# Three edits to the opening of an attention and MLP kernel: two product groups by contraction halves, key sums as a head of ones, and fewer idle products in fp32

## Chip, cores and metric

The kernel runs on one core of one Trainium2 chip. The metric is the device time of one execution in microseconds, as the median of several executions. The profile's span is about 1.8 us shorter than that time, because it runs from the first to the last recorded instruction of one profiled execution. Times of different kernels are compared only where they were measured on the same chip in the same rounds.

In this document, TensorE is called PE, VectorE DVE, ScalarE ACT, GpSimd POOL and SyncE SP. A load is one DMA transfer. The trace lists sixteen landings for it, one for each DMA engine; it counts as landed at the last of them, and the lag of an engine is how much later it lands than the other fifteen. Start to start is the time from the start of one product to the start of the next. The granted clock is the share of PE's full clock that the trace shows; "the gate opens" is its step from half to full.

## The reference

```python
# q, k, v: (8, 8, 576, 64) fp32; w_in (512, 2048), w_out (2048, 512) fp32
q_s = softmax(q over head_dim);  k_s = softmax(k over the sequence)
kv  = einsum('bhsd,bhse->bhde', k_s, v)          # one 64x64 matrix per head
x   = einsum('bhsd,bhde->bhse', q_s, kv)         # attention output
x   = x.transpose(0, 2, 1, 3).reshape(4608, 512) # tokens x d_model
h   = x @ w_in
g   = where(h > 0, h, exp(min(h, 0)) - 1)        # ELU
out = g @ w_out                                  # (4608, 512) fp32
```

## The kernel before

The program is laid out by a list scheduler of its own: each `S.add(engine, estimate, emit, key, ...)` names what an operation reads (`R`), writes (`W`) and both (`X`), and the scheduler orders each engine's instructions and places the semaphores. One unit is half of the heads of one batch, so batch 0 is units 0 and 1, and batch 1 is units 2 and 3. The 4608 tokens form nine blocks of 512.

The start-up matters here. The q loads of units 0 and 1 go first. Then one queue carries, in this order: k and v of units 0 and 1; sixteen pieces of w_in; then w_out in six pieces, mixed with q, k and v of units 2 and 3. The last things before the final two w_out pieces are the two halves of unit 3's v.

Meanwhile PE runs *idle products*, whose results nobody reads, so that its clock gate opens before the real work:

```python
def spin(self, count, bk, after=None):
    dst = self.bank(bk)
    def mm(e):
        for _ in range(count):
            last = e.matmul(dst, self.IDLE[:, 0:128], self.IDLE[:, :], start=True, stop=True)
        return last
    ...                                     # IDLE is 128 x 512, fp16
```

Unit 0's key sums (the softmax denominator over the sequence) are products of one column, ahead of the key-value products of 128 columns:

```python
def kz_first(self, n, ps, key):             # 18 products of one column each
    ...
                e.matmul(P[:, f * 512 + 128:f * 512 + 129], ek[fs, c, :], VB[fs, 0, c, D:D + 1], ...)
    ...                                     # then DVE takes the reciprocal

def kv_first(self, n, ps, key):             # 18 products of 128 columns each
    ...
                e.matmul(P[:, f * 512:f * 512 + 128], ek[fs, c, :], v[fs, :, c, :], ...)
    ...                                     # then DVE scales by the reciprocal into MBLK
```

A first-layer *group* g is 256 columns of d_ff for one block of 512 tokens: two tiles by four contraction pieces `kc`, which is eight products. A w_in load is one `kc` for four tiles, so groups 2 and 3 share four loads. In block 0, groups 0 and 1 are already split by contraction pieces, and group 2 in two halves:

```python
def hg(self, j, g, ps, key, how, kcs=(0, 1, 2, 3)):
    if (j, g) == (0, 2):
        self.hg_mm(j, g, ps, (0, 1), key)
        kcs = (2, 3)
    self.hg_mm(j, g, ps, kcs, key)
    ...                                     # exp on ACT, min and max on POOL/ACT/DVE into GT

def program(self):
    ...
    self.spin(10, 0)
    self.q_part(0, -90); self.q_mul(0, -90, None)
    self.spin(2, 0, "expq0"); self.spin(3, 0, "rec0")
    ...
    self.tp(0, 3, -84)                      # transposes of unit 0's q
    self.spin(4, 0); self.spin(2, 0, "rec1")
    self.kz_first(0, 2, -87); self.kv_first(0, 1, -87)
    ...
    for what in (0, "2q", "3q", 1, 2, "2k", "2v", "3k", 3, "3v", 4, 5):   # the queue after w_in
        ...
```

Block 0's second layer is woven with batch 1's attention. Its key-value products, `kv([2, 3])`, are one operation of 72 products that needs k and v of both units. It reads VB, the bf16 copy of v that DVE makes half by half.

The softmax here doesn't subtract the row's maximum and nothing guards it: scores larger than these inputs give would overflow.

Of the kernel before, what the change touches and what calls it, by code (L numbers as in the profile page):

```python
# [18 lines left out]
CH = 9  # L19
# [238 lines left out]
class Gen:  # L258
# [13 lines left out]
    def alloc(self):  # L272
        nc = self.nc
        a = nc.alloc_sbuf_tensor
        self.ID = a("ID", [128, 128], F16)
        self.IDLE = a("IDLE", [128, 512], F16)
        self.W1 = a("W1", [128, 4, DFF], F32R)
        self.W2 = a("W2", [128, 16, 512], F32R)
        self.GT = a("GT", [128, 16, BLK], F32R)
        self.XT = a("XT", [128, 4, RING], F32R)  # L280
        self.ESB = [a(f"ESB{i}", [128, 1024], F32) for i in range(4)]
        self.OSB = [a(f"OSB{i}", [128, 512], F32) for i in range(4)]
        self.RAW = [{t: a(f"{t.upper()}R{i}", [128, 2, CH, D], F32) for t in "kv"}
                    for i in range(2)]
        self.RQ = [a(f"QR{i}", [128, 2, CH, D], F32) for i in range(4)]
        self.VB = [a(f"VB{i}", [128, 2, CH, D + 1], BF16) for i in range(2)]
        self.QS = [a(f"QS{i}", [128, CH, 128], F16) for i in range(2)]
        self.qsT = [a(f"qsT{i}", [128, CH, 128], F32R) for i in range(2)]
        self.MB = a("MBLK", [128, 2, 2, 128], F32R)
        self.MBLK = [self.MB[:, i, :, :] for i in range(2)]  # L290
        self.ZQ = [a(f"ZQ{i}", [128, 2, CH], F32) for i in range(2)]
        self.RZQ = [a(f"RZQ{i}", [128, 2, CH], F32) for i in range(2)]
        self.RZ = a("RZK", [128, 2, 2], F32)
        self.RZK = [self.RZ[:, i, :] for i in range(2)]
        self.SEEN = a("SEEN", [16, 4, 16], F32)
        self.PS = [nc.alloc_psum_tensor(f"PS{i}", [128, 1024], F32) for i in range(4)]
# [10 lines left out]
    def load(self, n, t, eng, key, after=(), follow=None):  # L307

        b, u, i = n // 2, n % 2, n % (4 if t == "q" else 2)
        src = self.src[t][b, :, :, :].rearrange(  # L310
            "(h uf) (p c) d -> (uf p) h (c d)", h=2, c=CH)[128 * u:128 * u + 128]
        dst = self.raw(n, t)[:, :, :, :].rearrange("p h c d -> p h (c d)")
        if t == "v" and n < 2:
            dst = self.v16(n).rearrange("p h c d -> p h (c d)")
        return self.S.add(eng, ISSUE[eng], lambda e: e.dma_start(dst, src), key,  # L315
                          W=[f"{t}R{i}"] + (self.q_res(n - 4) if t == "q" and n in (4, 5) else []),
                          dma=f"{t}{i}{eng}", nbytes=128 * 4608,
                          after=after, follow=follow, low=True, tag=f"ld {t}{n}")

# [195 lines left out]
            ek[:, :, :, :], flat.rearrange("p (h c d) -> p h c d", h=2, c=CH), AF.Exp),  # L515
            key, X=[f"kR{n % 2}"], low=True, tag=f"expk{n}")

    def v16(self, n):

        return self.raw_flat(n, "v").bitcast(BF16)[:, 0:1152].rearrange(  # L520
            "p (h c d) -> p h c d", h=2, c=CH)

    def kz_first(self, n, ps, key):

# [12 lines left out]
        S.add("dve", 170, lambda e: e.reciprocal(rz.unsqueeze(2), PV[:, :, 128:129]), key,  # L537
              W=[f"RZK{n}"], X=self.banks(ps), tag=f"rzk{n}")

    def kv_first(self, n, ps, key):  # L540

        S = self.S
        P, ek, v, rz, M = self.PS[ps], self.ek2(n), self.v16(n), self.RZK[n], self.MBLK[n]

        def mm(e):
            for c in range(CH):
                for f in range(2):
                    fs = slice(f * 64, f * 64 + 64)
                    last = e.matmul(P[:, f * 512:f * 512 + 128], ek[fs, c, :], v[fs, :, c, :],
                                    start=(c == 0), stop=(c == CH - 1))  # L550
            return last
        S.add("pe", 470, mm, key, R=[f"kR{n}", f"vR{n}"], X=self.banks(ps), tag=f"kv{n}")
        PV = P[:, :].rearrange("p (f x) -> p f x", f=2)
        for h in range(2):
            hs = slice(h * 64, h * 64 + 64)
            S.add("dve", 290, lambda e, h=h, hs=hs: e.tensor_tensor(  # L556
                M[hs, :, :].rearrange("p f (e h) -> p f e h", h=2)[:, :, :, h], PV[hs, :, h * D:h * D + D],
                rz[hs, :].unsqueeze(2).broadcast_to([64, 2, D]), ALU.mult), key,
                R=[f"RZK{n}"], W=[f"MBLK{n}{h}"], X=self.banks(ps), tag=f"M{n}")
# [66 lines left out]



    def spin(self, count, bk, after=None):

        dst = self.bank(bk)

        def mm(e):
            for _ in range(count):
                last = e.matmul(dst, self.IDLE[:, 0:128], self.IDLE[:, :], start=True, stop=True)  # L635
            return last
        gate = [[o for o in self.S.ops if o.tag == after][-1]] if after else ()
        self.S.add("pe", count * 216, mm, -5, R=["IDLE"], X=[f"b{bk}"], after=gate, tag="spin")

    def hg_mm(self, j, g, ps, kcs, key=0):  # L640
        P = self.PS[ps]
# [14 lines left out]
    def hg(self, j, g, ps, key, how, kcs=(0, 1, 2, 3)):  # L656
        S = self.S
        P = self.PS[ps]
        if (j, g) == (0, 2):
            self.hg_mm(j, g, ps, (0, 1), key)  # L660
            kcs = (2, 3)
        self.hg_mm(j, g, ps, kcs, key)
        i = self.eslot % len(self.ESB)
        self.eslot += 1
# [59 lines left out]
    def init(self):  # L724
        S = self.S
        S.add("dve", 110, lambda e: e.memset(self.ID[:, :], 0.0), -95, W=["ID"])
        S.add("gp", 300, lambda e: e.affine_select(  # L727
            self.ID[:, :], self.ID[:, :], compare_op=ALU.not_equal, fill=1.0, base=0,
            pattern=[[-1, 128]], channel_multiplier=1), -79, X=["ID"])
        S.add("dve", 300, lambda e: e.memset(self.IDLE[:, :], 1.0), -96, W=["IDLE"])  # L730
        S.add("dve", 60, lambda e: e.memset(self.RZK[0], 0.0), -90, W=["RZK0"])
        for i in range(2):
            S.add("dve", 75, lambda e, i=i: e.memset(self.VB[i][:, :, :, D:D + 1], 1.0), -8,
                  W=[f"VBone{i}"])
            S.add("dve", 270, lambda e, i=i: e.memset(self.MBLK[i].bitcast(F32), 0.0), -8,
                  W=[f"MBLK{i}", f"MBLK{i}0", f"MBLK{i}1"])

    def program(self):
# [24 lines left out]
        for s in range(4):  # L763
            gp = self.load_w1(s, -60, follow=gp)
        S.add("act", 1400, lambda e: e.activation(
            self.RZK[0], self.RZK[0], AF.Exp), -65, X=["RZK0"])
        self.spin(10, 0)
        self.q_part(0, -90)
        self.q_mul(0, -90, None)
        self.spin(2, 0, "expq0")  # L770
        self.spin(3, 0, "rec0")
        self.q_part(1, -85)
        self.q_mul(1, -85, None)
        self.exp_k(0, -80)
        self.tp(0, 3, -84)
        self.spin(4, 0)
        self.spin(2, 0, "rec1")
        self.kz_first(0, 2, -87)
        self.kv_first(0, 1, -87)
        self.tp(1, 3, -84, evac="split")  # L780
        self.exp_k(1, -83)
        self.spin(2, 0)
# [45 lines left out]
        for j in range(NBLK):  # L828
            order = [A, Bs, C, Dd]
            for g in range(8):  # L830
                self.hg(j, g, order[g % 4], key, "gp" if j or g > 2 else "act" if g == 1 else "dve",
                        (0, 1, 2, 3) if j or g > 1 else (2, 3))
                key += 1
                if (j, g) == (0, 0):
                    elem_q(1, 8, None)
                    elem_k(1, 8, "dve")
# [92 lines left out]
```

## Time and profile before

| quantity | before |
|---|---|
| time, median of 3 executions | 298.55 us (298.37 to 298.98) |
| first w_in piece lands / first first-layer product | 13.14 / 13.28 us |
| first 16 KB instruction packet | 16.15 us |
| last half of unit 3's v lands | 42.46 us |
| batch 1's key-value products start | 43.01 us |
| from there to the end of the span | 253.79 us |

The page gives the busy time of an engine, its share of the span and its count of instructions. Of the profile before:

```profile
span 296.8 us, 4398 instructions
PE 291.0 (98%) x1852; PEld 234.9 (79%) x1852; DVE 149.9 (50%) x166; ACT 153.5 (52%) x182; POOL 122.7 (41%) x133
```

PE is the bound, so only PE's order, and what PE waits for, counts. A busy PE is not yet a useful PE: idle products count as busy.

### The profile page before, as it was taken

Reading aid. Unit: us, or ns where it says so; the run is one execution under the profiler, and the core shown is the slowest. Engines: PE = TensorE matmul, PEld = TensorE weight load, DVE = VectorE, ACT = ScalarE, POOL = GpSimd, SP = SyncE. Lnnn points to the kernel's source line nnn. Section 1 sums busy time; section 2 is a strip of 40 time slices with the busy share of each in tenths; the row PEclk is TensorE's granted clock in tenths of the full one; section 3 lists DMA queues with packets and bytes.
Section 4 is the critical chain, followed back from the end, with each engine's and each line's share of the span. In section 5 each row is a group of like instructions: output and inputs, shape, how many; then the busy total and the mean of one; then the engine's idle time right before and its main releaser. Section 6 shows DMA issues by size and latency. Waiting matters only on the chain.

```text
span 296.8 us, 4398 instructions
## 1 busy us (share of the span) xinstructions
PE 291.0 (98%) x1852; PEld 234.9 (79%) x1852; DVE 149.9 (50%) x166; ACT 153.5 (52%) x182; POOL 122.7 (41%) x133
## 2 busy tenths in 40 slices
PE   8999999999999999999999999999999999999995
PEld 2678778888888888888888888888888888888883
DVE  5766942988347903792268416760661056106600
ACT  5666367953776365546554745555534354125411
POOL 8998101652287035713472138315540055005500
PEclk9999999999999999999999999999999999999999
DMA  7999988928991696049902991099003110230022
GB/s 242 322 392 390 390 277 311 389 79 113 388 212 70 220 344 136 0 136 356 194 16 55 360 254 35 3 342 196 0 0 72 41 34 0 54 71 19 0 71 71
DMA packets 36515, 49.37 MB, mean 166 GB/s; under 512 B 16656, under 2 KB 17168, under 8 KB 36496
## 3 DMA queue, kind: packets, MB, share of 16 engines
q1 hardware_dynamic: 29792, 34.29, 41.1%
q0 software_dynamic: 6320, 14.29, 15.7%
q10 hardware_dynamic: 384, 0.53, 0.5%
q8 instruction: 14, 0.23, 0.3%
q14 instruction: 5, 0.04, 0.0%
HBM read 36.70 MB, written 9.44 MB: 155 GB/s over the span
## 4 chain that ended last, share of the span: by engine, by line
PE 84%; DMA 7%; POOL 7%; issue 0%; ACT 0%; DVE 0%; POOLq 0%
PE PS L698 41%; PE PS L649 39%; DMA VR<-in_v_dram 7%; POOL W L347 3%; PE PS L579 2%; PE PS L491 2%; POOL KR L315 1%; POOL W L358 1%; POOL VR L315 1%; POOL QR L315 0%; POOL QR L750 0%; ACT OSB L712 0%; DVE VB L442 0%; PE PS L613 0%; POOL ID L727 0%
## 5 line engine op out<-in xcount | busy, mean ns | idle before, releaser
L681 DVE SCALAR_TENSOR_TENSOR GT<-ESB,PS 128x1024 fp32r<-128x1024 f32 x69 | 84.1, 1220 | 116.0 <-POOL ESB L678 115.8
L698 PE MATMUL PS<-W,GT 128*128 128x512 f32 x576 | 139.9, 393 | 0.0
L649 PE MATMUL PS<-XT,W 128*128 128x512 f32 x576 | 133.0, 390 | 0.3 <-DMA W<-in_moe_w_in_dram 0.2
L649 PEld LDWEIGHTS PS<-XT,W 128*128 128x128 f32 x576 | 107.8, 188 | 23.3 <-DMA W<-in_moe_w_in_dram 0.6
L698 PEld LDWEIGHTS PS<-W,GT 128*128 128x128 f32 x576 | 106.2, 188 | 21.2 <-DMA W<-in_moe_w_out_dram 0.3
L678 POOL TENSOR_SCALAR ESB<-ESB 128x1024 f32<-128x1024 f32 x69 | 73.2, 1068 | 102.5 <-ACT ESB L666 102.5
L666 ACT ACTIVATE ESB<-PS 128x1024 f32<-128x1024 f32 x72 | 73.9, 1028 | 51.6 <-PE PS L649 51.6
L712 ACT ACTIVATE OSB<-PS 128x512 f32<-128x512 f32 x36 | 21.3, 599 | 63.0 <-PE PS L698 62.8
L438 POOL CAST VB<-VR 128x1152 bf16<-128x1152 f32 x12 | 14.4, 1202 | 45.8 <-DMA VR<-in_v_dram 45.8
L398 DVE TENSOR_REDUCE ZQ<-QR 128x18 f32<-128x1152 f32 (+1 forms) x18 | 21.8, 1214 | 3.0 <-ACT QR L392 3.0
L412 DVE TENSOR_TENSOR QS<-QR,RZQ 128x1152 f16<-128x1152 f32 x16 | 22.0, 1385 | 0.4
L599 ACT ACTIVATE XT<-PS 128x640 fp32r<-128x640 f32 (+3 forms) x24 | 15.6, 651 | 12.3 <-PE PS L579 12.3
L432 ACT ACTIVATE KR<-KR 128x1152 bf16<-128x1152 f32 x14 | 16.2, 1156 | 6.1 <-DMA KR<-in_k_dram 6.1
L392 ACT ACTIVATE QR<-QR 128x1152 f32<-128x1152 f32 (+1 forms) x18 | 18.4, 1052 | 1.7 <-DMA QR<-in_q_dram 1.6
L425 POOL CAST qsT<-QR 128x1152 fp32r<-128x1152 f16 x12 | 13.8, 1147 | 8.7 <-DMA QR<-QS 8.7
L579 PE MATMUL PS<-qsT,MBLK 128*128 128x320 f32 (+5 forms) x56 | 12.9, 312 | 0.0
L579 PEld LDWEIGHTS PS<-qsT,MBLK 128*128 128x128 f32 x56 | 10.5, 189 | 2.5 <-DVE MBLK L556 0.2
L635 PE MATMUL PS<-IDLE 128*128 128x512 f16 x24 | 8.8, 517 | 1.5 <-DVE IDLE L730 1.5
L358 POOL DMA_DIRECT2D W<-in_moe_w_out_dram x6 | 10.0, 2365 | 0.0
L347 POOL DMA_DIRECT2D W<-in_moe_w_in_dram x16 | 10.0, 1379 | 0.0
L635 PEld LDWEIGHTS PS<-IDLE 128*128 128x128 f16 x24 | 2.8, 125 | 6.2 <-issue 3.3
L491 PEld LDWEIGHTS PS<-VB,KR 64*64 64x64 bf16 x504 | 4.7, 107 | 2.8 <-DVE GT L681 1.8
(43 smaller groups left out, 70.2 us busy)
## 6 DMA issues: line engine op xcount, KB each, us to landing
out_dram<-OSB SPq DMA_DIRECT2D x68, 128.0 KB, 3.2
QR<-in_q_dram SPq DMA_DIRECT2D x12, 576.0 KB, 8.1
KR<-in_k_dram SPq DMA_DIRECT2D x12, 576.0 KB, 5.9
VR<-in_v_dram SPq DMA_DIRECT2D x12, 576.0 KB, 6.6
W<-in_moe_w_in_dram POOLq DMA_DIRECT2D x16, 256.0 KB, 9.9
W<-in_moe_w_out_dram POOLq DMA_DIRECT2D x3, 1024.0 KB, 16.8
KR<-in_k_dram POOLq DMA_DIRECT2D x4, 576.0 KB, 13.3
VR<-in_v_dram POOLq DMA_DIRECT2D x4, 288.0 KB, 14.5
```

The lines of the kernel that those rows point to most:

```text
L347: "gp", 530, lambda e, kc=kc: e.dma_start(self.W1[:, kc, sl], w[kc, :, :, sl]), key,
L392: lambda e, part=part: e.activation(part, part, AF.Exp), key,
L398: S.add("dve", 1350 if n > 1 else 750, lambda e, z=z, src=src: e.tensor_reduce(z, src, AX.X, ALU.add), key, R=self.q_res(n) if n > 1 else ...
L412: S.add("dve", 1400, lambda e: e.tensor_tensor(qso, raw[:, :, :, :], rz, ALU.mult), key, R=qR + [f"RZQ{i}"], W=[f"QS{al}"], low=True, tag= ...
L432: S.add("act", t_act(1152, False), lambda e: e.activation(ek[:, :, :, :], flat.rearrange("p (h c d) -> p h c d", h=2, c=CH), AF.Exp), key, ...
L579: return e.matmul(P[:, f * 512:f * 512 + n_], M[:, f, :], T[:, c0:c1, f * 64:f * 64 + 64], start=True, stop=True)
L649: last = e.matmul(P[:, t * 512:(t + 1) * 512], self.W1[:, kc, tt * 128:(tt + 1) * 128], self.XT[:, kc, rc:rc + BLK], start=(kc == 0), stop ...
L666: S.add("act", t_act(1024, True), lambda e: e.activation(esb[:, :], P[:, :], AF.Exp), key, W=[f"E{i}"], X=self.banks(ps), tag=f"exp{j}.{g}")
L678: S.add("gp", 1120, lambda e: e.tensor_scalar(esb[:, :], esb[:, :], 1.0, 0.0, ALU.min, ALU.max), key, X=[f"E{i}"], tag=f"min{j}.{g}", port ...
L681: S.add("dve", t_dve(1024), lambda e: e.scalar_tensor_tensor(gt, esb[:, :], -1.0, P[:, :], ALU.add, ALU.max), key, R=[f"E{i}"], W=gw, X=se ...
L698: last = e.matmul(dst, GT[:, jj, ts * 128:(ts + 1) * 128], self.W2[:, jj, :], start=(jj == 0), stop=(jj == 15))
L712: S.add("act", t_act(512, True), lambda e: e.activation(osb[:, :], src, AF.Copy), key, W=[f"O{i}0", f"O{i}1"], X=[f"b{bk}"], tag=f"evo{jb} ...
```

## The change

The change has three parts.

1. In block 0, groups 2 and 3 both go by contraction halves: first halves of 2 and 3, then second halves of 2 and 3. Each load gets more time before it is needed.
2. Unit 0's key sums become a third "head" of v that is all ones. The 18 one-column products disappear, and the key-value products grow from 128 to 192 columns.
3. Idle products are fp32. One of them is meant to hold PE as long as four fp16 ones. Fewer instructions then hold PE about equally long: 10 + 2 + 3 become 3 long ones and 1, and 4 become 1 long one.

PE's program shrinks from 1,852 to 1,820 products.

```diff
-        self.IDLE = a("IDLE", [128, 512], F16)
+        self.IDLE = a("IDLE", [128, 512], F32)
 ...
-    def kv_first(self, n, ps, key):
+    def kv_first(self, n, ps, key, sums=False):
+        w = 3 if sums else 2
-                    last = e.matmul(P[:, f * 512:f * 512 + 128], ek[fs, c, :], v[fs, :, c, :],
+                    last = e.matmul(P[:, f * 512:f * 512 + w * D], ek[fs, c, :], v[fs, 0:w, c, :],
+        if sums:
+            S.add("dve", 170, lambda e: e.reciprocal(rz.unsqueeze(2), PV[:, :, 128:129]), key, ...)
 ...
-        if (j, g) == (0, 2):
-            self.hg_mm(j, g, ps, (0, 1), key)
-            kcs = (2, 3)
 ...
+        S.add("dve", 300, lambda e: e.memset(self.v16(0, 3)[:, 2, :, :], 1.0), -8, W=["ones"])
 ...
-        self.spin(10, 0)
+        self.spin(3, 0, long=True)
-        self.spin(2, 0, "expq0")
-        self.spin(3, 0, "rec0")
+        self.spin(1, 0, "rec0")
-        self.spin(4, 0)
+        self.spin(1, 0, long=True)
-        self.kz_first(0, 2, -87)
-        self.kv_first(0, 1, -87)
+        self.kv_first(0, 1, -87, True)
 ...
-                        (0, 1, 2, 3) if j or g > 1 else (2, 3))
+                        (0, 1, 2, 3) if j or g > 3 else (2, 3))
+                if (j, g) == (0, 1):
+                    for x in (2, 3):
+                        self.hg_mm(0, x, order[x], (0, 1), key)
```

More of the change, by code (lines that the diff above doesn't have):

```diff
@@ L315, in load @@
         return self.S.add(eng, ISSUE[eng], lambda e: e.dma_start(dst, src), key,
-                          W=[f"{t}R{i}"] + (self.q_res(n - 4) if t == "q" and n in (4, 5) else []),
+                          W=[f"{t}R{i}"] + (["ones"] if t == "v" and n == 2 else []) + (self.q_res(n - 4) if t == "q" and n in (4, 5) else []),
                           dma=f"{t}{i}{eng}", nbytes=128 * 4608,
@@ L516, in exp_k, with v16 @@
             key, X=[f"kR{n % 2}"], low=True, tag=f"expk{n}")
-    def v16(self, n):
-        return self.raw_flat(n, "v").bitcast(BF16)[:, 0:1152].rearrange(
-            "p (h c d) -> p h c d", h=2, c=CH)
+    def v16(self, n, h=2):
+        return self.raw_flat(n, "v").bitcast(BF16)[:, 0:576 * h].rearrange(
+            "p (h c d) -> p h c d", h=h, c=CH)
     def kz_first(self, n, ps, key):
@@ L538, in kz_first @@
               W=[f"RZK{n}"], X=self.banks(ps), tag=f"rzk{n}")
-    def kv_first(self, n, ps, key):
+    def kv_first(self, n, ps, key, sums=False):
         S = self.S
-        P, ek, v, rz, M = self.PS[ps], self.ek2(n), self.v16(n), self.RZK[n], self.MBLK[n]
+        P, ek, v, rz, M = self.PS[ps], self.ek2(n), self.v16(n, 3), self.RZK[n], self.MBLK[n]
+        w = 3 if sums else 2
         def mm(e):
@@ L548, in mm @@
                     fs = slice(f * 64, f * 64 + 64)
-                    last = e.matmul(P[:, f * 512:f * 512 + 128], ek[fs, c, :], v[fs, :, c, :],
+                    last = e.matmul(P[:, f * 512:f * 512 + w * D], ek[fs, c, :], v[fs, 0:w, c, :],
                                     start=(c == 0), stop=(c == CH - 1))
             return last
-        S.add("pe", 470, mm, key, R=[f"kR{n}", f"vR{n}"], X=self.banks(ps), tag=f"kv{n}")
+        S.add("pe", 730 if sums else 500, mm, key, R=[f"kR{n}", f"vR{n}"] + (["ones"] if sums else []),
+              X=self.banks(ps), tag=f"kv{n}")
         PV = P[:, :].rearrange("p (f x) -> p f x", f=2)
+        if sums:
+            S.add("dve", 170, lambda e: e.reciprocal(rz.unsqueeze(2), PV[:, :, 128:129]), key,
+                  W=[f"RZK{n}"], X=self.banks(ps), tag=f"rzk{n}")
         for h in range(2):
@@ L625, in ao_last, with spin @@
               X=self.banks(ps), tag=f"evx{b}")
-    def spin(self, count, bk, after=None):
-        dst = self.bank(bk)
+    def spin(self, count, bk, after=None, long=False):
+        dst, idle = self.bank(bk), self.IDLE[:, :] if long else self.IDLE[:, 0:256].bitcast(F16)
         def mm(e):
             for _ in range(count):
-                last = e.matmul(dst, self.IDLE[:, 0:128], self.IDLE[:, :], start=True, stop=True)
+                last = e.matmul(dst, idle[:, 0:128], idle, start=True, stop=True)
             return last
         gate = [[o for o in self.S.ops if o.tag == after][-1]] if after else ()
-        self.S.add("pe", count * 216, mm, -5, R=["IDLE"], X=[f"b{bk}"], after=gate, tag="spin")
+        self.S.add("pe", count * (864 if long else 216), mm, -5, R=["IDLE"], X=[f"b{bk}"], after=gate, tag="spin")
     def hg_mm(self, j, g, ps, kcs, key=0):
```

## The prediction

> **What bounds the kernel now.** I read the page first (PE busy 291.0 of 296.8 us, granted clock at full in all 40 slices), then the chain that ended last in order of time, PE's timeline over the first 45 us, and the DMA issues stretch by stretch. The table of stretches shows where PE has slack. Its columns are the stretch, its length, busy time and count of PE, PEld, DVE, ACT and POOL, granted clock, DMA share and GB/s.
>
> ```profile
> 19.26:33.10 13.84, 13.84 (x61) 11.16 (x61) 10.90 (x10) 9.30 (x9) 10.61 (x14) 1.00 1.31 388
> 33.10:43.01 9.91, 9.64 (x57) 7.45 (x56) 6.59 (x9) 4.49 (x6) 0.00 (x0) 1.00 1.07 361
> 43.01:296.80 253.79, 250.12 (x1596) 206.37 (x1596) 120.79 (x123) 128.21 (x151) 93.93 (x88) 1.00 0.48 136
> ```
>
> After 43 us PE never waits (the missing 3.7 us are the last store). The change touches nothing there, so its whole worth is how much earlier PE reaches that point. What decides that is in the chain (start, length, what):
>
> ```profile
> 21.10 21.36 DMA VR<-in_v_dram
> 42.46 0.02 issue
> 42.49 0.48 DVE VB L442
> 42.96 0.04 issue
> 43.01 0.77 PE PS L491 x69
> ```
>
> The second batch's key-value products at 43.01 wait for the last half of unit 3's v, which lands at 42.46: the end of the load queue (about 390 GB/s from 15 us on), not PE's work, sets that time. PE's timeline shows the opening:
>
> ```profile
> 1.46 6.16 PE L635 MATMUL PS<-IDLE 128*128 128x512 f16 x15 [1.46 <-DVE IDLE L730]
> 7.51 0.68 PE L464 MATMUL PS<-ID,QS 128*128 128x128 f16 x9
> 8.03 1.72 PE L635 MATMUL PS<-IDLE 128*128 128x512 f16 x6
> 9.67 0.38 PE L532 MATMUL PS<-VB,KR 64*128 64x1 bf16 x18
> 9.91 0.66 PE L549 MATMUL PS<-VR,KR 64*128 64x128 bf16 x18
> ...
> 13.28 1.17 PE L649 MATMUL PS<-XT,W 128*128 128x512 f32 x4
> ...
> 19.26 10.29 PE L649 MATMUL PS<-XT,W 128*128 128x512 f32 x44 [0.21 <-DMA W<-in_moe_w_in_dram]
> ```
>
> The first-layer products start at 13.28. The first piece of w_in is issued at 5.69 and takes 7.5 us, so it lands near 13.2: this start too is set by a transfer. The wait of 0.21 at 19.26 is for group 2's second contraction half. The DMA issues of four stretches explain it (issues at 5.6 to 6.2, 8.6 to 9.2 and 9.2 to 9.8 us; last, the queues at 16.0 to 16.5 us):
>
> ```profile
> W<-in_moe_w_in_dram POOLq DMA_DIRECT2D x1, 256.0 KB, 7.5
> ...
> W<-in_moe_w_in_dram POOLq DMA_DIRECT2D x3, 256.0 KB, 8.2
> ...
> W<-in_moe_w_in_dram POOLq DMA_DIRECT2D x3, 256.0 KB, 9.7
> ...
> q8 instruction: 1, 0.02, 13.9%
> ```
>
> Pieces land every 0.68 us until 16.53; the next lands at 18.52. In between, at 16.15, one 16 KB instruction packet held one DMA engine for 1.11 us. The trace's sixteen landings of that piece run from 16.55 to 17.18 for fifteen engines and 18.52 for the sixteenth; the same gap of 1.38 us stays in every later load. The last half of v is complete on fourteen engines at 41.04 and on two at 42.42 and 42.46 (a second such packet came at 36.73). The same lag makes PE's weight loads wait at 33.09 for the second piece of w_out, which landed at 33.05:
>
> ```profile
> 33.09 2.61 PEld L698 LDWEIGHTS PS<-W,GT 128*128 128x128 f32 x12 [0.33 <-DMA W<-in_moe_w_out_dram]
> ```
>
> **What the Trainium skill says.** "Runtime: NRT & Kernel Launch", section "Instruction fetch mechanics": instructions come in 16 KiB blocks of 256. The trace agrees: 14 packets of 16 KB, by the trace's count 3,704 weight loads and products on PE, 265 for each packet. The page calls the cost "mostly hidden"; here it costs the loads 1.38 us. "DMA: Bandwidth & Descriptors", "Why a DMA increments its semaphore by 16 and not by 1": sixteen engines finish independently and a transfer counts only when all have; agreed, as above. "TensorE: Matmul & The Clock Gate", Part 1: a cold array runs at 1.2 GHz until a free-running window of 3.4 us has been busy. The trace agrees: idle products follow each other at 0.427 us up to 6.98, and at 0.216 from 8.03. "FP8 and Floating Point Precision", "TensorE Precision Notes": true fp32 takes four passes; no fp32 product with four passes is in this trace.
>
> **The change part by part.**
>
> *Idle products.* Removed: the first 10, the 2 after the exponentials of q, 2 of the 3 after the reciprocal, and 4 later ones. Added: 3 plus 1 in fp32. An estimate by the skill's four passes: one cold is 4 x 0.427 = 1.71 us, so three run from about 1.5 to 6.6, one more fp16 product to 7.07, and PE idles until the transposes at 7.51. They wait for DVE's QS, so they don't move. The later one, warm, is 4 x 0.216 = 0.86, as long as the four it replaces. The fill of 128x512 keeps its element count (0.48 us). Path: 0.
>
> *Key sums as a head of ones.* Removed: 18 products of one column, 0.24 us from start to start (9.67 to 9.91). Added: the 18 products grow from 128 to 192 columns. A pair of them takes 0.055 now; 192 columns at 2.4 GHz are 0.080, so nine pairs take 0.74 against 0.24 + 0.50 = 0.74: nothing on PE. But the reciprocal (0.16) now follows the products, where before it ran beside them: MBLK and the first attention products come some 0.2 us later (11.36 to about 11.6). Their copy into XT by DVE then ends near 12.85 instead of 12.63, still before 13.28; the second unit's products (12.26 to 13.1) may slip 0.1 and also still end before the first w_in piece. The new fill of ones (576 elements, estimated 0.6 us from the 0.48 of 512) falls into DVE's 2.1 us of idle time before 4.26. Path: 0.
>
> *Groups 2 and 3 by halves.* No product added or removed. The order shows 16 products before the second half of group 2 instead of 12, so PE gets there 4 x 0.23 = 0.92 later, at about 19.6, when those weights (19.22 in the worst case) are there. That removes a start-to-start gap of 0.60 where 0.23 is normal, and 0.11 of a slow second product: 0.48 us. Group 2's exponential moves about 0.4 later, with its PSUM not needed again before 25 us.
>
> *Instruction fetch.* PE's program has 1,820 products instead of 1,852, all 32 gone in the opening. With its weight load each, that is up to 64 instructions, so the first block boundary comes about 32 products later: at 0.23 each some 5 to 7 us, near 21 to 23 us (later pieces of w_in only). The second moves from 36.7 to about 44, past the last v.
>
> *Sum.* PE runs 0.48 ahead after 20 us. But at 33.09 it waits for w_out, at 43.01 for v. If the first fetch still falls before those loads, one engine still lags 1.38, and they still land at about 33.05 and 42.46. The gain becomes waiting. Products start at 43.0 as before: 0, and I allow 0.1 for a luckier engine. 298.55 - 0.1 = 298.45.
>
> **The rivals.**
> (a) The loads come early enough and the gain stays. The wait at 43.01 costs 0.66 from start to start where the later blocks show 0.32 at the same place, so at most 0.34 + 0.48 = 0.8 us: 297.7. For it: the second fetch leaves the queue's way, and the lagging engine could be one that is ahead by up to 0.6. Against: one lagging engine is enough, and already at 33.05 there was only one. Chance 15%.
> (b) The clock gate opens later because fp32 passes, or the 0.44 us gap before the transposes, count as less busy. A further 3.4 us of cold array would make idle products, transposes and the first sums 1 to 2 us longer and the first-layer start about 0.9 late. Of that the slack behind group 2 takes 0.48: 298.8 to 299.2. For: nothing in the trace of fp32. Against: the window that opened the gate, 3.6 to 7.0, is filled in both. Chance 10%.
> (c) The later reciprocal reaches the path: first-layer start 0.1 to 0.2 late, swallowed by the same two transfers. 298.5.
>
> **Range and chances.** The runs of before spread over 0.6 us (298.37 to 298.98), more than the change I expect. The 8-in-10 range takes half of rival (a) below and half of (b) above: 298.0 to 298.9. Two per cent are 6 us; the whole opening to which the change reaches has under 1 us of PE waiting to win, and a cold array costs about as much. Within 2%: 98%.
>
> **What would show it.** Right: no PE wait near 19 us; a single instruction packet between 19 and 25 us; first-layer products still at 13.2 to 13.4; PE waiting about 0.5 us longer near 33 or 43; last v near 42.4; kv products at 43.0. Wrong: last v landing before 42 (rival a), idle or transposing products at 0.1 us spacing after 7.5 us (rival b), or a first-layer start after 13.5 (c).

## The result, and the profile after

| | before (same rounds) | after |
|---|---|---|
| median | 298.73 us | 298.61 us |
| lowest to highest of 4 fast runs each | 298.37 to 298.98 | 298.16 to 298.78 |
| ratio, 95% interval | | 0.9995 (0.9977 to 1.0012) |

Ratios are the mean time of one kernel's fast runs over that of the other's in the same rounds, so they are not quite the ratio of the medians quoted. The change is within 2%, and no difference between the two kernels is resolved. The measured 298.61 us lies in the predicted range of 298.0 to 298.9, and 0.16 us above the predicted 298.45. The runs of one kernel spread over 0.6 us, so that closeness is partly luck: what the result supports is "no change", not the 0.1 us of gain.

The page of the changed kernel:

```profile
span 297.0 us, 4343 instructions
PE 289.8 (98%) x1824; PEld 234.7 (79%) x1824; DVE 150.7 (51%) x167; ACT 153.5 (52%) x182; POOL 123.0 (41%) x133
```

PE is 1.2 us less busy and the span is not shorter. The trace counts 28 fewer products where the program has 32 fewer. PE's timeline of the opening shows why. The columns are start, length from first to last, engine, line, operation, output and inputs, shapes, count and the idle time before.

```profile
1.46 4.35 PE L640 MATMUL PS<-IDLE 128*128 128x512 f32 x6 [1.46 <-DVE IDLE L732]
6.35 0.39 PE L640 MATMUL PS<-IDLE 128*128 128x512 f16 x1 [0.54 <-DVE RZQ L401]
7.75 0.68 PE L464 MATMUL PS<-ID,QS 128*128 128x128 f16 x9 [1.00 <-DVE QS L412]
...
10.05 0.92 PE L550 MATMUL PS<-VR,KR 64*128 64x192 bf16 x18
...
13.82 1.17 PE L654 MATMUL PS<-XT,W 128*128 128x512 f32 x4
16.58 13.17 PE L654 MATMUL PS<-XT,W 128*128 128x512 f32 x56
```

Three fp32 idle products are six records in the trace. While cold, each record took 0.853 us, so one product took 1.71 us. The key-value products of 192 columns stand where the sums were. The first-layer products then run from 16.58 to 29.75 in one piece: the wait at 19.26 of before is gone from this list. Start to start, small gaps of 0.328 and 0.307 us remain at group 4, where 0.23 is normal.

The first-layer start is later: 13.82 against 13.28. The chain that ended last, in order of time, then goes through the same load as before:

```profile
21.15 21.47 DMA VR<-in_v_dram
42.62 0.02 issue
42.65 0.48 DVE VB L442
43.13 0.04 issue
43.17 0.78 PE PS L491 x67
```

The last half of unit 3's v lands at 42.62 (42.46 before), DVE converts it, and the key-value products start at 43.17 (43.01 before). The table of stretches (stretch, length, then busy time and count of PE, PEld, DVE, ACT and POOL, granted clock, DMA share, GB/s) closes the account:

```profile
33.10:43.17 10.07, 9.86 (x56) 7.46 (x55) 6.79 (x9) 4.49 (x6) 0.00 (x0) 1.00 1.05 355
43.17:297.00 253.83, 250.16 (x1596) 206.40 (x1596) 120.47 (x123) 128.20 (x151) 94.09 (x88) 1.00 0.47 136
```

The stretch after the key-value products takes 253.83 us (253.79 before) with the same 1596 products. PE is busy 9.86 of 10.07 us ahead of them.

One thing did move. The first 16 KB instruction packet came at 17.78 us instead of 16.15, and the second at 42.02 instead of 36.73. The list of DMA queues of the changed kernel from 17.5 to 18 us has it (queue: packets, MB, share of the time):

```profile
q8 instruction: 1, 0.02, 14.4%
```

The lag of one DMA engine behind the others moved with the first packet. In the profile before it appears at w_in piece 7, complete on 15 engines at 17.18 and on the last at 18.52. In the changed kernel it appears at piece 9: 19.06 and 20.10.

### The profile page after: what moved, and what is told of

The parts are those of the page before. It is cut to its first block, busy times and chain, and to the rows that moved or that the text cites. A ratio compares the mean times of both kernels' runs of the same rounds, so it can differ in the third digit from the quotient of the medians.

```text
span 297.0 us, 4343 instructions
## 1 busy us (share of the span) xinstructions
PE 289.8 (98%) x1824; PEld 234.7 (79%) x1824; DVE 150.7 (51%) x167; ACT 153.5 (52%) x182; POOL 123.0 (41%) x133
## 4 chain that ended last, share of the span: by engine, by line
PE 84%; DMA 7%; POOL 7%; issue 0%; ACT 0%; DVE 0%; POOLq 0%
PE PS L700 41%; PE PS L654 39%; DMA VR<-in_v_dram 7%; POOL W L347 3%; PE PS L584 2%; PE PS L491 2%; POOL KR L315 1%; POOL W L358 1%; POOL VR L315 1%; POOL QR L315 0%; POOL QR L753 0%; ACT OSB L714 0%; DVE VB L442 0%; PE PS L618 0%; POOL ID L729 0%
## 5 line engine op out<-in xcount | busy, mean ns | idle before, releaser
L640 PE MATMUL PS<-IDLE 128*128 128x512 f32 (+1 forms) x14 | 7.4, 632 | 2.0 <-DVE IDLE L732 1.5
L640 PEld LDWEIGHTS PS<-IDLE 128*128 128x128 f32 (+1 forms) x14 | 2.5, 199 | 5.8 <-DVE RZQ L401 2.2
```

## The experiments

The theory: the key-value products of batch 1 start at the later of two times, the landing of the last half of unit 3's v plus about 0.55 us, and the time that PE itself needs from the first first-layer product. None of the three parts moves the later of the two. The main rival: the parts do change something, but their effects cancel (for example, a gain from the halves against a loss from the later start or from the clock gate).

Twelve runs were made in two sets, each set on one chip; e10 repeats after, e11 repeats e1 and e12 repeats before. The kernel before had a median of 299.06 us in the first set (e1 to e4) and 298.94 us in the second (e5 to e12). Medians of different sets are not compared. All results passed the comparison with the reference. That includes e5 and e6, which were computed from wrong data; so the comparison does not see that data, or tolerates it.

All profiled executions fit in one table. "PE's own" is the time from the first first-layer product to the key-value products. "Wait" is the start-to-start gap ahead of the key-value products, which is 0.32 where nothing is waited for. In e7 and e9, the key-value start is that of unit 2's own products.

| run | 1st instr. packet | first-layer start | last v lands | kv start | wait | PE's own | kv to end | median us |
|---|---|---|---|---|---|---|---|---|
| before | 16.15 | 13.28 | 42.46 | 43.01 | 0.66 | 29.73 | 253.8 | 298.73 |
| after | 17.78 | 13.82 | 42.62 | 43.17 | 0.60 | 29.35 | 253.8 | 298.61 |
| e1 halves | 17.99 | 16.03 | 42.45 | 44.69 | 0.32 | 28.66 | 254.0 | 298.75 |
| e2 idle products | 19.84 | 16.71 | 42.22 | 45.34 | 0.32 | 28.63 | 253.9 | 298.95 |
| e3 ones | 17.48 | 13.96 | 42.97 | 43.51 | 0.58 | 29.55 | 254.0 | 298.81 |
| e4 more idle | 14.94 | 13.82 | 42.59 | 43.13 | 0.62 | 29.31 | 254.0 | 298.89 |
| e5 light, before | 16.44 | 13.73 | 41.09 | 42.38 | 0.32 | 28.65 | 253.8 | 298.18 |
| e6 light, after | 17.21 | 13.69 | 41.22 | 42.70 | 0.32 | 29.01 | 253.8 | 298.25 |
| e7 split, after | 17.35 | 13.67 | 42.35 | 42.59 | 0.32 | 28.92 | 254.1 | 298.54 |
| e8 no idle, after | 20.37 | 14.66 | 41.84 | 43.32 | 0.32 | 28.66 | 254.0 | 299.00 |
| e9 split, before | 17.05 | 13.51 | 42.10 | 42.42 | 0.32 | 28.91 | 254.0 | 298.35 |
| e10 after again | 17.78 | 13.60 | 42.21 | 42.76 | 0.64 | 29.16 | 253.8 | 298.73 |
| e11 halves again | 16.37 | 13.30 | 42.58 | 43.13 | 0.62 | 29.83 | 253.8 | 298.71 |
| e12 before again | 16.29 | 13.25 | 42.55 | 43.09 | 0.73 | 29.84 | 253.8 | 298.69 (one run) |

Where the wait is above 0.32, the key-value products start 0.54 to 0.55 us after the landing of v. In e1, e2, e5 and e8, where it is 0.32, they start 28.63 to 28.66 us after the first first-layer product. That is PE's floor when it waits for no load on the way. In e6, e7 and e9 it is 0.32 too, but smaller gaps on the way make it 28.91 to 29.01. The intervals of the ratios are as wide as the whole prize, so the times alone could not show what a part does; the traces have to.

### e1: the halves alone

```diff
# before, with the reordering of groups 2 and 3 and nothing else (cut)
+                if (j, g) == (0, 1):
+                    for x in (2, 3):
+                        self.hg_mm(0, x, order[x], (0, 1), key)
```

> The kernel before with only groups 2 and 3 by contraction halves; idle products and key sums as before. My theory (the loads set when PE reaches 43 us): the instruction packet still comes near 16.1 us, the wait before group 2's second half (0.21 us idle, 0.48 lost) is gone, but the lagging engine now makes PE wait at group 4 (its weights land near 21.9, PE is there near 21.6), so less than 0.3 us is kept, and that is lost again at 33.05 (second piece of w_out) and before the key-value products, which start at 43.0 plus or minus 0.2. Time 298.3 to 298.9, ratio 0.999 to 1.001. Rival (PE's gain is kept): key-value products near 42.5, time near 298.1.

Measured: 298.75 us median, ratio 0.9996 (0.9977 to 1.0015). The profile fell into an unusual execution (300.51 us; the others took 298.54 to 299.01). There, the second half of unit 0's q landed at 6.27 us instead of 4.27 (fifteen DMA engines were done at 4.35, one at 6.27), and PE's timeline shows what that did:

```profile
7.03 0.61 PE L635 MATMUL PS<-IDLE 128*128 128x512 f16 x2 [1.42 <-ACT QR L392]
9.51 1.14 PE L464 MATMUL PS<-ID,QS 128*128 128x128 f16 x9 [0.36 <-DVE QS L412]
16.03 1.20 PE L649 MATMUL PS<-XT,W 128*128 128x512 f32 x4
```

PE had an idle time of 1.42 us. The granted clock, full from 5.19, was half from 8.60 to 12.01, and nine transposes took 1.14 us instead of 0.68. The first-layer products began 2.1 us after their weights had landed (13.90). This is rival (b) of the prediction in full, yet in a kernel that still has all 24 fp16 idle products. It also shows a useful limit: with PE 2.75 us late at 16.03, all waits for loads vanish and the key-value products are only 1.68 us later than in the profile before. The halves themselves could not be judged on this profile, so they were run again as e11.

### e2: the fp32 idle products alone

```diff
# shortened
-        self.IDLE = a("IDLE", [128, 512], F16)
+        self.IDLE = a("IDLE", [128, 512], F32)
-        self.spin(10, 0)           # and spin(2, "expq0"), spin(3, "rec0"), spin(4)
+        self.spin(3, 0, long=True) # and spin(1, "rec0"), spin(1, long=True)
```

> The kernel before with only the idle products changed (fp32, fewer). My theory: PE idles 0.5 to 1.0 us before the first transposes, and this costs nothing, because the first-layer products wait for the first piece of w_in (start within 0.2 us of its landing). The program is 10 pairs of weight load and product shorter, so the first instruction packet comes up to 1 us later than 16.1. Key-value products at 43.0 plus or minus 0.2, time 298.3 to 298.9. Rival (the clock gate opens later with less idle work): transposes 0.1 us apart instead of 0.056, first-layer start more than 0.4 us after the landing, time above 299.0.

Measured: 298.95 us, ratio 1.0016 (0.9979 to 1.0053). Again the profile fell on an unusual execution (301.06 us) with q late (6.42 us, fifteen engines at 4.43) and PE idle for 1.52 us; the gate closed again from 9.83 to 13.25, and first-layer products began at 16.71. The rival's symptom is there. But e1 has the same symptom without the fp32 products, and both have the late q. So this trace does not speak against the fp32 products. The other executions, at 298.74 to 298.97, do not either. The median is just above the expected 298.3 to 298.9, and the rest of the expectation (packet up to 1 us later, key-value products near 43.0) could not be judged: no ordinary profile of the idle products alone was taken. After and e10, which have all three parts, stand in for it.

### e3: the head of ones alone

```diff
-        self.kz_first(0, 2, -87)
-        self.kv_first(0, 1, -87)
+        self.kv_first(0, 1, -87, True)
+        S.add("dve", 300, lambda e: e.memset(self.v16(0, 3)[:, 2, :, :], 1.0), -8, W=["ones"])
```

> The kernel before with only the first unit's key sums beside its products. My theory: its 18 products take as long as the 36 they replace (0.7 to 0.8 us from first to last start plus one), the reciprocal comes after them and the first attention products about 0.2 us later measured from the landing of v, and the first-layer products still start within 0.2 us of the landing of the first piece of w_in. Time 298.3 to 298.9. Rival (the later reciprocal reaches the path): first-layer start 0.3 us or more after that landing, time 298.8 to 299.1.

Measured: 298.81 us, ratio 0.9996 (0.9977 to 1.0015). The expectation was met. The first-layer start was 13.96, which is 0.14 after its weights landed (13.82), as in before (13.14 and 13.28). The later reciprocal is therefore not on the path. A wait of 0.531 us remained at group 2, and the key-value products started 0.54 after v.

### e4: more idle products instead of fewer

```diff
-            for _ in range(count):
-                last = e.matmul(dst, self.IDLE[:, 0:128], self.IDLE[:, :], ...)
+            for _ in range(4 * count if count == 10 else count):
+                n = 128 if count == 10 else 512
+                last = e.matmul(dst[:, 0:n], self.IDLE[:, 0:128], self.IDLE[:, 0:n], ...)
```

> The kernel before with its first ten idle products of 512 columns as forty of 128: the same columns, 60 more instructions. My theory (a 16 KB instruction packet holds one DMA engine and every later load lands some 1.1 to 1.4 us late on that one): the packet comes earlier, at 12 to 15 us, and the lag of one engine begins at the first w_in piece that lands after it, not at the seventh; PE then waits for an early w_in piece and not, or less, at group 2; key-value products again at 43.0 plus or minus 0.2 since one engine lags by then in either kernel; time 298.4 to 299.0. Rival (the lag comes from something else, such as the order of the loads): it still begins at the seventh piece near 16.5 to 18.5 us.

Measured: 298.89 us, ratio 1.0000 (0.9983 to 1.0016). With 30 products more, the instruction packet came at 14.94 and the lag of one DMA engine began at w_in piece 5 (16.04 on 15 engines, 17.06 on the last), two pieces earlier than in before. The wait near 20 us was gone: all products from 16.61 on ran in one piece.

```profile
16.61 12.95 PE L650 MATMUL PS<-XT,W 128*128 128x512 f32 x56
43.13 0.78 PE L491 MATMUL PS<-VB,KR 64*64 64x65 bf16 x72 [0.23 <-DVE VB L442]
```

The w_in piece that group 2 waits for in before (the eighth) landed 5.19 us after the first-layer start here, against 5.94 in before. Instead, PE waited more at the second w_out piece (a gap of 0.467 at 33.27, 0.297 in before). So the lag follows the packet, and the place of the wait changes with it. The start at 43.13 and the time did not move. Whether the packet comes earlier or later, the v loads at the end of the queue have the lag behind them.

### e5 and e6: lighter loads, on before and on after

Half of q of units 2 and 3 (2 x 288 KB) is not loaded, and its place is filled by DVE. The result is wrong there.

```diff
+        if t == "q" and n in (2, 3):
+            src, dst = src[:, 0:1, :], dst[:, 0:1, :]
+        for i in (2, 3):
+            S.add("dve", 600, lambda e, i=i: e.memset(self.RQ[i][:, 1, :, :], 0.1), -8, W=[f"qR{i}"])
```

> The kernel before with only half of q of units 2 and 3 loaded in the early queue (the rest filled with a constant; a wrong result on purpose): 0.59 MB or about 1.5 us less ahead of the second piece of w_out and of the last v. My theory: last v lands near 41.0, PE no longer waits near 33 or 43 us, the key-value products start where PE gets to them, about 29.2 us after the first first-layer product (before: 29.7), and the time falls by 0.3 to 0.6 us. Rival (PE is not held by these loads): no change.

Measured for e5: 298.18 us against 298.94, ratio 0.998 (0.9962 to 0.9998), somewhat more than the 0.3 to 0.6 us expected. v landed at 41.09, which would allow 41.64. The chain no longer goes through v: it runs along PE from the first-layer products to the key-value products without a load between them.

```profile
16.64 12.86 PE PS L651 x56
29.49 6.34 PE PS L700 x28
...
42.45 0.70 PE PS L493 x68
```

The key-value products start at 42.38, 28.65 after the first-layer start (pieces of the chain do not overlap, so it lists 42.45). This is the size of the whole prize: 0.63 us of start against the profile before and 0.71 against e12, and 0.76 us of median (298.94 - 298.18); the interval of the ratio allows 0.1 to 1.1 us. The second w_out piece came earlier too (31.46 instead of 33.05), so e5 tests the queue of loads as a whole and not v alone.

> The changed kernel with the same lighter load of q (wrong result on purpose). My theory: here the 0.4 to 0.5 us that the change saves near group 2 can show: the key-value products start 28.7 to 28.9 us after the first first-layer product, 0.3 to 0.5 less than in the lighter kernel before, and the time is 0.2 to 0.5 us below that one's. Rival (the change saves nothing even where the loads are out of the way, because with the later instruction packet or without the lag there was nothing to save): the same interval and time as the lighter kernel before.

Measured for e6: 298.25 us, ratio 0.9975 (0.9961 to 0.9989), so no faster than e5. The rival was right here: with the loads out of the way, the change brings nothing on top. Its chain shows why:

```profile
16.61 5.56 PE PS L656 x24
22.17 0.13 issue
22.30 7.50 PE PS L656 x32
```

The wait that the halves take from group 2 stands at group 4 (a start-to-start gap of 0.518), after 24 products instead of after 12. In e5, group 2 had not waited at all: its last piece landed 5.39 us after the first-layer start, against 5.94 in before. There was nothing left to save.

### e7 and e9: unit 2's key-value products do not wait for unit 3's v

Here one operation of 72 products becomes two of 36, each with its own waits, on after (e7) and on before (e9).

```diff
+            if units == [2, 3] and n == 2:
+                S.add("pe", 370, lambda e: whole(e, 2), key, R=R, X=self.banks(ps), tag="kv2")
+                R, mm = [], lambda e: whole(e, 3)
```

> The changed kernel with the second batch's key-value products as two blocks, unit 2 first and unit 3 with a wait of its own, so that only unit 3's 36 products wait for the last v. My theory: unit 2's products run in the time in which PE now waits (start near 42.5), unit 3's at 43.0 to 43.2 as the last v lands, and the output products after them start 0.3 to 0.4 us earlier; time 298.1 to 298.4. Rival (the wait is not what holds the end): no change, 298.6.

Measured for e7: 298.54 us, ratio 0.9998 (0.9971 to 1.0026; one of its executions took 301.2), above the 298.1 to 298.4 expected. The output products after them started at 43.35. In before, after and e10 they start 1.25 to 1.26 us after the last v landed, which here would be 42.35 + 1.26 = 43.61. So the split moved them 0.26 earlier, where 0.3 to 0.4 had been expected, and no gain in time is resolved.

> The kernel before (none of the change) with the second batch's key-value products in two blocks. If the changed kernel's own parts save nothing and the split is what helps, this one does as well as the changed kernel with the split: unit 2's products while the last v is still on its way, the output products after them 0.7 to 0.9 us after the last landing instead of 1.25 (43.72 - 42.46 in the kernel before), median 0.2 to 0.5 us below the kernel before. If the change contributes, this one stays within 0.1 us of the kernel before.

Measured for e9: 298.35 us against 298.94, ratio 0.999 (0.9971 to 1.0009; five runs at 298.19 to 298.78 and one at 299.78). The output products follow at once:

```profile
42.42 0.84 PE L493 MATMUL PS<-VB,KR 64*64 64x65 bf16 x72
43.19 1.66 PE L703 MATMUL PS<-W,GT 128*128 128x512 f32 x6
```

43.19 is 0.17 earlier than 42.10 + 1.26 = 43.36; the rest of what it gains over before (43.72) comes from v landing earlier in this execution. It is 1.09 after the last landing where 0.7 to 0.9 had been expected: PE itself reached unit 2's products only at 42.42. By the median, e9 is the best correct version, and it has none of the change. The interval includes 1, so that it beats both kernels is likely rather than shown.

### e8: no idle products at all

```diff
     def spin(self, count, bk, after=None, long=False):
+        return
```

> The changed kernel without any idle product. My theory: PE is cold until well after the first-layer products begin; transposes 0.11 us apart, first-layer products 0.43 apart for 3 to 7 us, first-layer start 0.5 to 1.5 us late, and PE loses 2 to 4 us of which only about 0.5 is covered by the waits near 33 and 43 us: time 300 to 303. If idle products are worth nothing here: 298.6, which would say that the loads cover all of it.

Measured: 299.00 us, ratio 1.0006 (0.9983 to 1.0028). This expectation failed: 300 to 303 had been expected. PE's timeline:

```profile
7.58 1.14 PE L464 MATMUL PS<-ID,QS 128*128 128x128 f16 x9 [7.58 <-DVE QS L412]
14.66 1.20 PE L655 MATMUL PS<-XT,W 128*128 128x512 f32 x4
```

The whole attention opening ran cold, and the gate opened at 14.65, just as the first-layer products began. These were 1.4 us later than their weights' landing (13.26). But PE then waited for no load, and reached the key-value products at 43.32, which is 0.15 later than in the profile after. So no cost of leaving the idle products out is resolved; the interval allows up to 0.8 us. In this profile, most of what a cold opening costs would have been spent waiting for the loads anyway.

### e10, e11 and e12: the changed kernel, the halves alone and the kernel before, again

> The changed kernel once more, for a second trace and a narrower interval. Theory: ratio within 0.998 to 1.001; key-value products start at the later of two times, 0.55 us after the last v lands, or PE's own 28.7 to 29.1 us after the first first-layer product; the end 253.8 to 254.0 us after them.

> The halves alone once more, because the first look fell into an execution whose q came late and whose clock gate closed again (2 us late, no wait left to see). Theory for an ordinary execution: no wait at group 2, a wait of 0.1 to 0.5 us at group 4 if the lagging engine's pieces land after 21.8 us, key-value products 0.55 us after the last v; time 298.4 to 299.1. Rival (the halves keep their gain): key-value products more than 0.3 us earlier than the kernel before's in the same call and no wait before them.

> The kernel before once more, one look: how much the opening moves by itself. Theory: the first landings of w_in and with them the first first-layer product move by up to 0.5 us (13.3 to 13.8) from run to run, the clock gate opens anywhere between 4.5 and 8 us, the wait at group 2 is there only if the first-layer start is early against the lagging engine; key-value products 0.55 us after the last v lands, the end 253.8 to 254.0 us later.

The times were 298.73, 298.71 and 298.69 us. The expectations were met, but for two narrow misses: e10's ratio is 1.0012 (0.9987 to 1.0037) where 1.001 was the upper end, and e12's first-layer start is 13.25 where 13.3 was the lower. Their ordinary profiles show the halves' effect by itself. First e12 (before), then e11 (halves):

```profile
16.00 2.99 PE L649 MATMUL PS<-XT,W 128*128 128x512 f32 x12
19.27 10.31 PE L649 MATMUL PS<-XT,W 128*128 128x512 f32 x44 [0.27 <-DMA W<-in_moe_w_in_dram]
```

```profile
16.06 5.73 PE L649 MATMUL PS<-XT,W 128*128 128x512 f32 x24
22.17 7.54 PE L649 MATMUL PS<-XT,W 128*128 128x512 f32 x32 [0.39 <-DMA W<-in_moe_w_in_dram]
```

With the halves, 24 products run before the wait instead of 12, but the wait is still there, at 22.17 instead of 19.27. Start to start it is 0.773 at group 4 instead of 0.656 at group 2. PE's own time up to the key-value products is the same, 29.83 against 29.84.

In after, the gap at group 4 is only 0.328, and in e10 it is gone. The piece waited for there is the twelfth of w_in. It landed at 22.08 in e11, at 22.12 in after and at 21.68 in e10. Counted from the first-layer start, that is 8.78, 8.30 and 8.08 us. So the wait in after is smaller mainly because PE started 0.52 later than in e11, not because the piece came earlier. In e10 it is some of both (0.30 later, 0.40 earlier). The order of the groups is the same in all three, so it does not explain the difference.

## Why the prediction was right

**The sum.** The prediction's main step was that a gain before 33 us becomes waiting, because the key-value products at 43 us wait for v. That is what all ordinary profiles show. Of the signs that it named, the missing wait near 19 us, the landing of v (42.62) and the start at 43.17 came true; the packet's time, the first-layer start and the longer wait did not, and are taken up below. In before, after, e3, e4, e10, e11 and e12 the key-value products start 0.54 to 0.55 us after v's last half landed, whatever PE had won or lost before. e5 is the test of the reason itself: with less to load, the same PE program starts them at 42.38 and the median falls by 0.76. Rival (a) had put the prize at 0.8 at most. It was right about its size, but the change does not collect it.

**Idle products.** The estimate of 1.71 us for a cold fp32 product was right, 2 x 0.853. In e10, three ran from 1.45 to 6.73 as worked out, and the gap before the transposes was 0.37 (0.44 had been worked out). Rival (b), a gate that opens later, did not occur in ordinary executions: it opened at 4.53 in after and 7.00 in e10, against 7.06 in before and 6.27 in e12. What did occur, in e1 and e2, is a gate that closed again when q came late. That cost up to 2.8 us at the first-layer start, and it is not confined to the fp32 products, since e1 has none. In both, a single DMA engine brought its share of q 1.9 to 2.0 us after the other fifteen; why is open. Executions above 300 us were 3 of 25 in kernels with the fp32 idle products (one each of e2, e7 and e10) and 1 of about 52 in kernels with the fp16 ones (e8, which has none, is not counted). A mean granted clock of 0.994, which e1 and e2 have, marks 4 of those 25 and 2 of the 49 whose clock is on record. That suggests a longer tail with the changed idle products. It doesn't show it. The traces point the same way. If the windows of 3.41 us seen in e1 and e2 run on from the opening of the gate, PE was busy in the first one after it for 44% in e1 and 26% in e2, where the gate then closed. It was 55% in after and 60% in e6, where it opened early as well (4.53 and 4.59) and stayed open, against 77% in e5 and e11 (4.94 and 5.04) and 61% in e4 with its forty short products (4.86). Rival (b) asked only about the window that opens the gate; where the gate opens early, the change leaves the next one thinner.

**Key sums.** The estimate of 0.74 for 18 products of 192 columns was right, though nine times the 0.080 from which it came is 0.72: a pair took 0.084 on the mean, which gives 0.76. The first attention product starts 1.83 us after these products start (after and e10) instead of 1.69 after the sums start (before and e12), so the delay is 0.14 where 0.2 had been predicted, and it is off the path. The symptom named for rival (c), a first-layer start after 13.5, did appear (13.82 and 13.60), but from another cause: in the ordinary profiles (all but e1, e2 and e8, whose opening ran cold, and e4, where the gap was 0.44) the start is 0.13 to 0.14 after the first w_in piece landed, and that landing varied between 13.11 and 13.82. The piece was issued at 5.68 to 5.71 in all of them. The first k landed between 8.06 and 8.90, and w_in 4.9 to 5.2 after it, so the variation comes in with the earlier transfers. A start after 13.5 also appears without the ones (13.73 in e5, 13.51 in e9). Whether the fill of ones adds to it is not settled.

**Groups by halves: a step that failed.** "PE runs 0.48 ahead after 20 us" was read from the group-2 wait alone. The order of groups only moved that wait to group 4 (0.656 to 0.773, with PE's own time 29.84 and 29.83). The mistake was to ask whether the weights of group 2's second half were in time, and not to ask the same of the next piece in the queue. If every later piece lands late by the same lag, PE meets the lag at the next group that has no slack. This did not spoil the sum, because what it would have given was written off.

**Instruction fetch: a term that was mis-sized.** The first packet was expected at 21 to 23 us, 5 to 7 us later; it came at 17.78, 1.6 later. (By the prediction's own figures, 32 products at 0.23 are 7.4.) The direction was right, and e3 (1.3 later) and e4 (1.2 earlier with 30 products more) agree with it, but the first packet does not follow the count of products. Counted in the traces, 131 products had started in before when it came, 107 in after and 151 in e4. So of the 28 records that after lacks, it moved by only 4; the late first-layer start is another 0.54 us. The second packet does follow the count, with 209 to 228 products started in all fourteen profiles: 36.73 to 42.02 is 5.3 us, against an estimate of 28 x 0.23 = 6.4, where 44 had been predicted. Why the first one does not is not shown by any run. Moving the second packet away would not have freed v: the lag of one engine was there from the first packet on (1.04 us at w_in piece 9, 0.89 at a v load that landed at 38.98) and still at the last v (41.77 on 15 engines, 42.62 on the last).

**PE waiting 0.5 longer near 33 or 43.** This did not appear: the wait at the key-value products was 0.60 in after and 0.64 in e10, against 0.66 and 0.73. PE did wait less on the way, but it had also started its first layer 0.3 to 0.6 us later than in the two profiles before (13.60 and 13.82 against 13.25 and 13.28), so it did not arrive earlier by as much. PE's own time shrank by 0.38 to 0.68 us (29.73 and 29.84 to 29.35 and 29.16), which is that later start, plus or minus the landing of v.

**The Trainium skill.** "Runtime: NRT & Kernel Launch", section "Instruction fetch mechanics", explained most: it led to the 16 KB packets among the loads. Its "mostly hidden" is true of PE here, which does not stop for the packet. It is not true of the loads behind it. "DMA: Bandwidth & Descriptors", "Why a DMA increments its semaphore by 16 and not by 1", agrees: the lag of one engine of sixteen delays every transfer's completion.

## What to carry to other kernels

Before you value the removal of a wait, ask which later wait will end at the same time whether or not the engine comes early: here the last v at 42.5 us, behind which no gain of the three parts was to be measured, while lighter loads gave 0.76 us. If a wait is due to a queue that lags, a new order of the consumer can move the wait to a later piece, as from 19.27 to 22.17 here; look there before counting the gain. And measure what the warming work is worth by leaving it out: in e8 a cold opening hid almost whole behind the loads, while a gate that closed again (e1, e2) cost about 2 us.

## What the Trainium skill lacked or had wrong

- "Runtime: NRT & Kernel Launch", "Instruction fetch mechanics", calls the cost of a 16 KiB boundary "mostly hidden". Here one such packet held a DMA engine for 1.11 us, and from then on later loads landed 0.8 to 1.4 us later on one engine (0.8 in e10, 1.4 in before) than on the others. The page does not say that fetch shares the engines with the kernel's own loads.
- "FP8 and Floating Point Precision", "TensorE Precision Notes", gives four passes for true fp32. The runs agree on the time (1.71 us cold against 4 x 0.427), and add that the trace has two records for each such product, of 0.853 us each, so a count of records overstates the program by one for each.
- "TensorE: Matmul & The Clock Gate", Part 1, under "HAM oscillation — how this bites in real kernels", gives the abstract rule "no PE-idle gaps >~3.4µs". In e1 and e2 the gate closed again for a window of 3.41 us where the longest idle time was 1.42 and 1.52 us, with shorter ones beside it; all idle time in the window before it closed was 1.9 us (e1) and 2.5 us (e2) of 3.41. The page's next section tells of a gate that oscillates on short idle times, but has no figure for how much idle time closes it. In other executions it opened at 4.5 to 7.1 us for nearly the same program.
